# Recurrent attention and a token and channel mixer: padded 512-byte weight pieces, fp32 sums in batch 0, halves read in place, and a stored order table

## The chip, the cores and the metric

The kernel runs on one core of a Trainium2 chip. The metric is the device time of one execution in microseconds (us), from the runs shown below; a trace of one further execution shows what each engine did. The engines are TensorE (PE, with its weight loads as PEld), VectorE (DVE), ScalarE (ACT), GpSimd (POOL) and SyncE (SP), which here only issues transfers (DMAs).

## The reference

There are 4 batches of 768 tokens, with 8 heads of 48 columns, so 384 model columns. Per head a state of 48 by 48 decays by a gate and takes up an outer product at every token:

```python
f = 1.0 / (1.0 + np.exp(-f_logit))
state = f[:, :, t, :, None] * state + np.einsum('bhd,bhe->bhde', k[:, :, t], v[:, :, t])
y[:, :, t] = np.einsum('bhd,bhde->bhe', q[:, :, t], state)
```

The result, heads side by side, is x. It goes through two mixings, first over the tokens and then over the channels:

```python
h = np.maximum(xt @ w_tok1, 0.0) @ w_tok2      # xt: x transposed, hidden 256
u = x + h.transpose(0, 2, 1)
return u + np.maximum(u @ w_ch1, 0.0) @ w_ch2  # hidden 1536
```

All inputs and outputs are fp32.

## The kernel before, in words

**Attention.** Each batch is cut into three chunks of 256 tokens, called b,d (batch, chunk). Two neighbouring tokens lie side by side in one partition (index j in 0, 1), so a chunk fills 128 partitions, and e in 0, 1 names the two halves of 64 partitions. The recurrence is computed in blocks, as masked attention inside a block and a carried state between blocks. For each chunk, with line numbers of the kernel before:

- f is loaded; exp and ln(1 + x) on ACT (L536, L538) give minus the logarithm of the gate. P (L543, DVE) adds the two tokens of a pair into the tile Pf in fp32.
- Pf is split into two bf16 parts: hi, a cast (L545), and lo, the remainder (L547). TensorE forms the running sums of both with a triangular matrix of ones (`cums`, L552: L556 for hi, L557 for lo), and the totals of each half with eight small matmuls (L561, L562). S0 (L566, DVE) takes the second token's value off to get the sums for the first token of each pair.
- G and Gi (L577, L579, ACT) are the exponentials of minus and plus the sums; q and k are multiplied with them ("gating", L607 and L618), transposed on TensorE (L641) or, in batches 2 and 3, by a transposing DMA (L653), and copied out.
- TensorE computes scores (L769, or L725 in batches 2 and 3), DVE multiplies them with a mask (L776, L733), TensorE multiplies with v (L786, L740) and adds the carried state's part (L798, L749). The result is copied to x (L823), and to bf16 for the mixing.

**Mixing.** Token mixing takes two groups of matmuls, tok1 (L839) and tok2 (L855), with the sum u added in place by DVE (L861). u is cast to bf16, transposed on TensorE (L876), and channel mixing follows for two halves of 384 tokens: ch1 (L902) with a relu to the tiles z on ACT or DVE (L909, L911), and ch2 (L927), 12 matmuls into one PSUM bank for each of six tiles of 128 tokens, added to u by DVE (L937). Two stores (L946) put a pair of tiles out, one for each half of the partitions; the last two tiles are stored singly.

**Loads.** SP issues q, k, v and f in one queue, in pieces of 384 bytes (two tokens of one head), into five buffers for each of the four. Behind batch 0's loads stand the token weights in fp32: w1 (L446) in pieces of 2 KB into its own tile w1s, then w2 (L458) in two halves of 3 KB pieces, which borrow one buffer of v and one of k. ACT, POOL and DVE cast them to bf16. The channel weights are loaded, with a cast on the way, in four transfers that POOL issues (L470, L474). The first waits behind a gate (L435) for w2's second half, the third for a load of q of batch 1.

**Order.** Nothing is ordered by hand. Every piece of work is registered with a `Planner`, with its planned time on each engine that may do it, its inputs and outputs, its buffers and a priority. The planner plays the program through: of all work that is ready it takes what can start first by its own clock, and of equal starts the one with the lower priority value (L153). This gives each engine its instruction order, chooses engines and buffers, and is fixed before the kernel runs. The priorities come from due times: 34 us per batch (`due`, `at`, L351 to L373). Where TensorE would idle before 60 us by the plan, filler matmuls on a constant tile (`idle`, L983) are put in; they compute nothing. The PSUM has eight banks; one is kept for fillers until 26 us by the plan (`P.spare`).

Of the kernel before, what the change touches and what calls it, by code (L numbers as in the profile page):

```python
# [12 lines left out]

SEM = 0.06
PE_LAT = 0.10
SW_LEAD, HW_LEAD = 3.9, 3.7


def act_t(n):
    return (0.05 + 0.835e-3 * n, 0.12)  # L20

# [8 lines left out]

def pe_mode(name):

    if name.startswith("sc"):
        return "s"
    if name.startswith("ds"):
        return "d"
    return "v" if name.startswith("av0") else "n"
# [7 lines left out]
class Planner:  # L45


    def __init__(self):
        self.ops, self.by_name = [], {}
        self.pools, self.group_pool, self.group_of = {}, {}, {}  # L50
        self.producers, self.touch = {}, {}
        self.bank_pools, self.banks, self.quota, self.warm = {}, [], None, 0.0
        self.held, self.spare, self.slack, self.patience = [], 0.0, {}, 0.0
# [33 lines left out]
    def run(self):  # L87
# [31 lines left out]
        while ready:  # L119
            best = None  # L120
            cache = {size: self._banks(size) for size in (1, 2)}
            for o in ready:
# [23 lines left out]
                for e, (occ, lat) in o.eng.items():  # L146
# [6 lines left out]
                    key = (round(st + self.patience * max(o.prio, -20.0), 2), o.prio, st + occ)  # L153
# [17 lines left out]
            if o.xfer is not None and e == "POOL":  # L171
# [12 lines left out]
                end = sw + 0.3  # L184
# [50 lines left out]
    def switch(a, b):  # L235
        if a == b:
            return 0.0
        return (0.095 if a == "s" else 0.0) + (0.093 if b != "n" and a != "s" else 0.0)
# [22 lines left out]
def kernel(  # L261
# [23 lines left out]
    XB_FROM = 2  # L285
    DEEP = 2
# [28 lines left out]
    Pf_tiles = [st([128, H, D], FP32, f"Pf{i}") for i in range(2)]  # L315
    P.pool("Pf", Pf_tiles)
    L_tiles = [(st([128, H, 64], BF16, f"Phi{i}"), st([128, H, 64], BF16, f"Plo{i}")) for i in range(2)]
    P.pool("L", L_tiles)
    P.pool("U", [st([128, 2, DM], BF16, f"v_bf{i}") for i in range(3)])
# [8 lines left out]
    idle = st([128, 512], BF16, "idle")  # L328
# [18 lines left out]
    P.patience = 0.0  # L347
    P.spare = 26.0
# [29 lines left out]
    def consts():  # L378
# [4 lines left out]
        for hi, lo in L_tiles:  # L383
            nc.vector.memset(hi[:, :, D:64], 0.0)
            nc.vector.memset(lo[:, :, D:64], 0.0)
        nc.vector.memset(halves, 0.0)
# [6 lines left out]
        nc.vector.tensor_scalar(tri2[0:64, 0:64], tri[0:64, 0:64], -1.0, None, ALU.add)  # L393
        for r in (slice(0, 64), slice(64, 128)):
# [13 lines left out]
    def load(nm, b, d, prio, after=()):  # L408
# [4 lines left out]
             prio, after, xfer=ROW * 128 * H)  # L413

    for b in range(B):
        seq = [(nm, c + 1 if nm == "f" else c) for c in range(-1, NP) for nm in "fqkv"]
        if b == 0:
            seq = [(w[0], int(w[1])) for w in "f0 f1 q0 k0 f2 v0 q1 k1 v1 q2 k2 v2".split()]
# [8 lines left out]
    gates = dict(zip(("wc1a", "wc1b", "wc2a", "wc2b"), ("w2s1", "-", "q1,1", "-")))  # L427
    sw = []

    def sw_dma(nm, outs, fn, n, mb):  # L430
        dep = ["~" + sw[-1]] if sw else []
        at_ = gates.get(nm, "-")
        if at_ != "-":
            P.op(f"gate_{nm}", {"POOL": (0.13, 0.1)}, [at_], [],
                 lambda: nc.gpsimd.tensor_copy(gate_t, P[at_][:, 0, 0, 0:1]), -900 + len(sw), dep)  # L435
            dep = ["~gate_" + nm]
        P.op(nm, {"POOL": (0.7 * n, 0)}, [], outs, fn, -899.5 + len(sw), dep, xfer=mb / 0.31)
        sw.append(nm)
    w1s = st([128, 3, 2, DT], FP32, "w1s")

    def flat(v):
        return P[v].rearrange("p h two d -> p (h two d)")
    tail = f"~ldv0,{NP - 1}"
    for n in range(2):
        P.value(f"w2s{n}", f"w2s{n}", "vk"[n])
    P.op("w1l", {"SP": (0.7, 0)}, [], ["w1s"], lambda: nc.sync.dma_start(  # L446
        out=w1s.rearrange("p g two c -> p g (two c)"),
        in_=moe_w_tok1.rearrange("(g p two) c -> p g (two c)", p=128, two=2)), -400, [tail], xfer=0.786 / 0.35)
    tail = "~w1l"
    for j in range(2):  # L450
        for kk in range(2):
            P.op(f"w1c{j},{kk}", {"POOL": pool_t(768), "ACT": act_t(768)}, ["w1s"], [f"w1{kk}"],
                 lambda e, j=j, kk=kk: cast(
                     e, w_tok1[64 * j:64 * j + 64].rearrange("p (g kk) c -> p kk g c", kk=2)[:, kk],
                     w1s[64 * kk:64 * kk + 64, :, j]), T0 - LEAD - 4 + kk)
    for kt in range(2):
        P.op(f"w2l{kt}", {"SP": (0.7, 0)}, [], [f"w2s{kt}"],
             lambda kt=kt: nc.sync.dma_start(out=flat(f"w2s{kt}"), in_=moe_w_tok2[128 * kt:128 * kt + 128]),  # L458
             -390 + kt, [tail], xfer=0.393 / 0.35)
        tail = f"~w2l{kt}"  # L460
        for th in range(2):
            P.op(f"w2{kt},{th}", {"ACT": act_t(384), "DVE": dve_t(384)}, [f"w2s{kt}"], [f"w2{th}"],
                 lambda e, kt=kt, th=th: cast(
                     e, w_tok2[:, kt, 384 * th:384 * th + 384].rearrange("r (c two p) -> r c two p", two=2, p=64),
                     flat(f"w2s{kt}")[:, 384 * th:384 * th + 384].rearrange(
                         "r (c p two) -> r c two p", p=64, two=2)), T0 - LEAD - 2 + th)
    P.by_name["ldf1,0"].after = (tail,)
    for hf in range(2):
        cols = slice(hf * (DCH // 2), (hf + 1) * (DCH // 2))
        sw_dma("wc1" + "ab"[hf], ["wc1" + "ab"[hf]], lambda cols=cols: nc.gpsimd.dma_start(  # L470
# [550 lines left out]
```

## Time and profile before

The median of 4 runs is 185.09 us (184.31 to 185.58). The profiled execution is one of them.

| | us |
|---|---|
| profiled execution | 185.58 |
| its span, first to last instruction | 183.8 |
| TensorE busy (93%) | 170.8 |
| of it fillers, L983 | 20.7 |
| DVE busy (66%) | 121.5 |
| ACT busy (65%) | 119.7 |
| POOL busy (37%) | 68.0 |

The core moved 31.00 MB at 169 GB/s on average. In the rows shown below, a line such as L902 is a line of the kernel; "out<-in" are tiles with their numbers left out; "issue" is time in which an engine waited for nothing that the profile shows. A share of busy time is an average over stages with different limits, so the stages are read one by one. The chain of waits follows the work that ended last back to the start, in order of time: start, duration, what.

### The profile page before, as it was taken

To read this page: it belongs to the slowest core of one execution; us is meant where nothing else is said; L and a number is where in the kernel's file an instruction comes from. 1 tells how busy PE (TensorE), PEld (TensorE's weight loads), DVE (VectorE), ACT (ScalarE), POOL (GpSimd) and SP (SyncE) were. 2 spreads that over 40 slices of the span, in tenths; PEclk is the share of its full clock that TensorE was granted. 3 is DMA by queue.
4 is the path that set the end of the run, shared out by engine and by line. 5 is a ranking of instruction groups with operands and counts; after the bars stand their busy time and mean duration, and the time that the engine had idled before them with its cause. 6 is when DMAs were issued, how large, how long until landed. Compare 5 with 4: busy or idle time off the path is not lost.

```text
span 183.8 us, 5042 instructions
## 1 busy us (share of the span) xinstructions
PE 170.8 (93%) x2050; PEld 105.9 (58%) x2050; DVE 121.5 (66%) x232; ACT 119.7 (65%) x215; POOL 68.0 (37%) x114
## 2 busy tenths in 40 slices
PE   6899969999999999999989999889999999999990
PEld 2346645575666766565656665356666666566650
DVE  7489865598857688998489996998944266012021
ACT  3879689899766688767777945368337542924800
POOL 3017872375274337385642934437210100000000
PEclk9999997999999999999999999999999999999999
DMA  6999999979993999999999899995352011303033
GB/s 151 261 261 263 294 327 234 209 181 272 209 206 80 278 241 271 205 181 166 207 281 229 176 244 195 198 203 85 44 84 75 0 42 47 86 0 87 4 90 81
DMA packets 69159, 31.00 MB, mean 169 GB/s; under 512 B 63120, under 2 KB 68496, under 8 KB 69136
## 3 DMA queue, kind: packets, MB, share of 16 engines
q1 hardware_dynamic: 66768, 28.32, 72.9%
q0 software_dynamic: 2368, 2.36, 7.7%
q8 instruction: 16, 0.26, 0.6%
q14 instruction: 7, 0.06, 0.1%
HBM read 25.17 MB, written 4.72 MB: 163 GB/s over the span
## 4 chain that ended last, share of the span: by engine, by line
PE 65%; DVE 14%; ACT 7%; SPq 5%; DMA 3%; issue 3%; DVEq 0%; ACTq 0%
PE pp L902 24%; PE pp L927 21%; SPq L412 5%; DVE qkh L618 3%; DMA v_ld<-in_v_dram 3%; DVE xu L861 3%; PE pp L855 2%; PE pp L798 2%; DVE qkh L607 2%; ACT xu L823 2%; PE pp L725 2%; PE pp L839 2%; PE pp L786 2%; PE pp L769 2%; PE pp L641 2%
## 5 line engine op out<-in xcount | busy, mean ns | idle before, releaser
L927 PE MATMUL pp<-w_ch,zT 128*128 128x384 bf16 x288 | 52.2, 326 | 0.0
L902 PE MATMUL pp<-uT,w_ch 128*128 128x384 bf16 x288 | 51.5, 326 | 0.6 <-DVE zT L911 0.4
L909 ACT ACTIVATE zT<-pp 128x384 bf16<-128x384 f32 x72 | 34.9, 491 | 18.1 <-PE pp L902 17.9
L902 PEld LDWEIGHTS <-w_ch 128*128 128x128 bf16 x288 | 26.9, 98 | 17.2 <-issue 1.0
L927 PEld LDWEIGHTS <-zT 128*128 128x128 bf16 x288 | 27.0, 98 | 16.5 <-issue 0.2
L937 DVE TENSOR_TENSOR xu<-xu,pp 128x384 f32<-128x384 f32 x24 | 13.3, 552 | 29.2 <-PE pp L927 29.0
L481 POOL CAST v_bf<-v_ld 64x384 bf16<-64x384 f32 (+1 forms) x28 | 16.2, 579 | 19.4 <-DMA v_ld<-in_v_dram 18.3
L983 PE MATMUL pp<-idle 128*128 128x512 bf16 (+4 forms) x82 | 20.7, 338 | 1.5 <-DVE idle L379 1.5
L776 DVE TENSOR_TENSOR AmT<-pp,msk 128x1024 bf16<-128x1024 f32 x12 | 14.4, 1221 | 3.4 <-PE pp L769 2.1
L911 DVE TENSOR_SCALAR zT<-pp 128x384 bf16<-128x384 f32 x24 | 12.7, 555 | 4.6 <-PE pp L902 3.7
L733 DVE TENSOR_TENSOR AmT<-pp,msk 128x1024 bf16<-128x1024 f32 x12 | 14.1, 1218 | 2.4 <-PE pp L725 2.3
L481 POOL CAST x_bf<-xu 128x768 bf16<-128x768 f32 x10 | 8.5, 852 | 17.7 <-ACT xu L823 17.7
L607 POOL TENSOR_TENSOR qkh<-q_ld,G 128x384 bf16<-128x384 f32 x14 | 13.0, 940 | 2.4 <-ACT glast L574 2.2
L618 DVE TENSOR_TENSOR qkh<-k_ld,pp 64x384 bf16<-64x384 f32 x24 | 13.2, 550 | 0.5
L983 PEld LDWEIGHTS <-idle 128*128 128x128 bf16 x82 | 7.9, 104 | 8.2 <-issue 2.8
L536 ACT ACTIVATE f_ld<-f_ld 128x768 f32<-128x768 f32 x12 | 10.1, 840 | 3.4 <-DMA f_ld<-in_f_logit_dram 3.4
L861 DVE TENSOR_TENSOR xu<-xu,pp 128x384 f32<-128x384 f32 x24 | 11.7, 548 | 0.2 <-PE pp L855 0.2
L548 POOL TENSOR_TENSOR Plo<-Pf,Phi 128x384 bf16<-128x384 f32 x10 | 9.1, 913 | 6.9 <-ACT Phi L479 3.0
L823 ACT COPY xu<-pp 128x768 f32<-128x768 f32 x11 | 8.8, 797 | 4.3 <-PE pp L786 2.3
L577 ACT ACTIVATE G<-pp 128x768 bf16<-128x768 f32 x12 | 9.7, 812 | 2.7 <-DVE pp L566 2.6
L839 PE MATMUL pp<-x_bf,w_tok 128*128 128x384 bf16 x48 | 10.0, 340 | 0.8 <-ACT w_tok L479 0.4
L479 ACT CAST u_bf<-xu 128x768 bf16<-128x768 f32 x8 | 6.5, 831 | 6.3 <-DVE xu L861 6.1
(99 smaller groups left out, 249.1 us busy)
## 6 DMA issues: line engine op xcount, KB each, us to landing
f_ld<-in_f_logit_dram SPq DMA_DIRECT2D x12, 384.0 KB, 5.4
q_ld<-in_q_dram SPq DMA_DIRECT2D x12, 384.0 KB, 6.3
k_ld<-in_k_dram SPq DMA_DIRECT2D x12, 384.0 KB, 6.2
v_ld<-in_v_dram SPq DMA_DIRECT2D x12, 384.0 KB, 6.9
out_dram<-xu SPq DMA_DIRECT2D x22, 192.0 KB, 2.9
w_ch<-in_moe_w_ch_dram POOLq DMA_DIRECT2D x4, 576.0 KB, 9.3
w1s<-in_moe_w_tok_dram SPq DMA_DIRECT2D x1, 768.0 KB, 7.9
v_ld<-in_moe_w_tok_dram SPq DMA_DIRECT2D x1, 384.0 KB, 6.1
```

What stands on the lines that cost most here:

```text
L481: (nc.vector if e == "DVE" else nc.gpsimd).tensor_copy(o, x)
L607: vec(e).tensor_tensor(o, x, g, ALU.mult)
L618: nc.vector.tensor_tensor(o, x, g, ALU.mult)
L733: lambda e=e: nc.vector.tensor_tensor(P[f"Am{e}{i}"], P[f"A{e}{i}"].rearrange("p b (a t) -> p (b a) t", t=128), msk2.rearrange("p j t -> p ...
L776: lambda j=j: nc.vector.tensor_tensor(P[f"Am{j}{i}"], P[f"A{j}{i}"].rearrange("p b (a t) -> p (b a) t", t=128), msk[:, j].rearrange("p j t ...
L839: nc.tensor.matmul(P[f"{g},0"][:, 0:DM], lhsT=w_tok1[:, kt, rt * 128:(rt + 1) * 128], rhs=P[f"xb{b},{kt // 2}"][:, kt % 2], start=(kt == 0 ...
L861: nc.vector.tensor_tensor(x, x, P[f"up{i}"][:, 0:DM], ALU.add)
L902: nc.tensor.matmul(pm, lhsT=w_ch1[:, kt, cc * 128:(cc + 1) * 128], rhs=uT[:, 3 * th:3 * th + 3, kt, :], start=(kt == 0), stop=(kt == 2))
L909: nc.scalar.activation(P[f"z{i}"], P[f"zp{i}"][:, 0:384], AF.Relu)
L927: nc.tensor.matmul(P[f"op{i}"][:, 0:DM], lhsT=P[f"z{b},{th},{cc}"][:, c0:c0 + 128], rhs=w_ch2[:, cc, :], start=(cc == 0), stop=(cc == NCC ...
L937: nc.vector.tensor_tensor(x, x, P[f"op{i}"][:, 0:DM], ALU.add)
L983: nc.tensor.matmul(P.psum_tile[:, bank, 0:n], lhsT=idle[:, 0:128], rhs=idle[:, 0:n], start=True, stop=True)
```

## The change

- **Order.** A table of 967 integers, `RANKS`, replaces the priorities of all registered work, in order of registration. The planner is otherwise the same, with new planned times for several operations (`act_s`, the transposes, the copies of the state, transfers), and keeps a bank for fillers until 30.
- **Token weights.** w1 is loaded by three DMAs, w2 by two, in 512-byte pieces into tiles whose rows are padded from 128 to 132 columns. w2 has its own tile and no longer borrows buffers.
- **Upper halves.** hi is no longer cast: it is the upper 16 bits of Pf, read in place with a step of two bf16 elements. The tiles Phi go, Pf is 64 columns per head.
- **fp32 sums.** In chunks 1 and 2 of batch 0 (`f32p`) the sums are formed by fp32 matmuls from Pf; hi, lo and S0 go there. `minus_ln` starts the first token's sums with minus the second token's value.
- **Tail.** The last tile's ch2 is done in two halves of 192 columns, each with its add. The stores of the last two tiles go out on two queues, SP and ACT.
- **Fillers.** The constant tile is 128 columns; 64 of them are repeated to the filler's width.

Flags that are 0 (`F32`, `WSW`, `COLS`) leave their branches unused. The diff, cut to its core:

```diff
+RANKS = """
+560 561 562 563 564 565 566 567 568 569 570 571 573 574 575 576 577 578 579 580 581 582 583 584 587 588 589 590 591
...
-SW_LEAD, HW_LEAD = 3.9, 3.7
+SW_LEAD, SW_END, HW_LEAD = 2.4, 2.3, 3.7
+def act_s(n):
+    return (0.095 + 0.835e-3 * n, 0.12)
-                    key = (round(st + self.patience * max(o.prio, -20.0), 2), o.prio, st + occ)
+                    key = (int(st * 100.0 + 0.5), o.prio, st + occ)
-                end = sw + 0.3
+                end = sw + SW_END
...
+    HIV = 1
+    F32P = 2
-    Pf_tiles = [st([128, H, D], FP32, f"Pf{i}") for i in range(2)]
+    Pf_tiles = [st([128, H, 64 if HIV else D], FP32, f"Pf{i}") for i in range(2)]
-    idle = st([128, 512], BF16, "idle")
+    idle = st([128, 128], BF16, "idle")
-    P.spare = 26.0
+    P.spare = 30.0
...
+        if F32 or F32P:
+            nc.vector.tensor_copy(tri2f[:, 0], tri2)
+            nc.vector.tensor_copy(halvesf, halves)
+        if F32P:
+            nc.vector.tensor_scalar(tri2f[:, 1], ident, -1.0, None, ALU.mult)
...
-    w1s = st([128, 3, 2, DT], FP32, "w1s")
+        w1s = st([128, 3, 4, 132], FP32, "w1s")
+        def w1_load():
+            for g in range(3):
+                nc.sync.dma_start(out=w1s[:, g, :, 0:128], in_=moe_w_tok1.rearrange(
+                    "(g p two) (ch c) -> g p (two ch) c", p=128, two=2, ch=2)[g])
+        P.op("w1l", {"SP": (1.4, 0)}, [], ["w1s"], w1_load, -400, [tail], xfer=0.786 / 0.33)
...
-             lambda kt=kt: nc.sync.dma_start(out=flat(f"w2s{kt}"), in_=moe_w_tok2[128 * kt:128 * kt + 128]),
+        w2s = st([128, 2, 6, 132], FP32, "w2s")
+                 lambda kt=kt: nc.sync.dma_start(
+                     out=w2s[:, kt, :, 0:128], in_=moe_w_tok2[128 * kt:128 * kt + 128].rearrange("r (c x) -> r c x", x=128)),
...
+        f32p = F32P and b == 0 and d >= F32P - 1
+        def hi_of():
+            if HIV:
+                return P[f"Pf{i}"].bitcast(BF16).rearrange("p h (d two) -> p h d two", two=2)[:, :, :, 1]
+            return P[f"L{i}"][0]
-        P.op(f"hi{i}", {"POOL": pool_t(384), "ACT": act_t(384)}, [f"Pf{i}"], [f"hi{i}"],
+        if not HIV and not f32:
+          P.op(f"hi{i}", {"POOL": pool_t(384), "ACT": act_s(384)}, [f"Pf{i}"], [f"hi{i}"],
...
-            hi, lo = P[f"L{i}"]
+            hi, lo = hi_of(), P[f"L{i}"][1]
+        def minus_ln():
+            nc.tensor.matmul(hd(P[f"S{i}"][:, 0, 0:DM]), lhsT=tri2f[:, 1], rhs=f_()[:, :, 1], start=True, stop=False,
+                             skip_group_check=True)
+
+        def cums32p():
+            x = P[f"Pf{i}"]
+            for a in (1, 0):
+                nc.tensor.matmul(hd(P[f"S{i}"][:, a, 0:DM]), lhsT=tri2f[:, 0], rhs=x[:, :, 0:D], start=(a == 1),
+                                 stop=(a == 0), skip_group_check=True)
+
+        def totals32p():
+            o, x = P[f"S{i}"][:, 1], blk(P[f"Pf{i}"])
+            for hp in range(HP):
+                nc.tensor.matmul(o[:, DM + 2 * hp:DM + 2 * hp + 2], lhsT=x[:, hp], rhs=halvesf, start=False,
+                                 stop=(hp == HP - 1), skip_group_check=True)
+        if f32p:
+            P.op(f"mln{i}", {"PE": (0.65, PE_LAT)}, [f"Ln{i}"], [f"S0{i}"], minus_ln, pg - 3.6)
+            P.op(f"cums{i}", {"PE": (1.3, PE_LAT)}, [f"Pf{i}", f"S0{i}"], [f"S{i}", f"Sa{i}"], cums32p, pg - 3.5)
+            P.op(f"cumt{i}", {"PE": (0.5, PE_LAT)}, [f"Pf{i}", f"Sa{i}"], [f"S1{i}"], totals32p, pg - 3.4)
...
+            if b == B - 1 and tt == NCH - 1:
+                for n in range(2):
+                    c = slice(n * (DM // 2), (n + 1) * (DM // 2))
+                        def ch2(tt=tt, g=g, i=i, th=th, c=c, n=n):
+                            for cc in range(g * 3, g * 3 + 3):
+                                nc.tensor.matmul(P[f"op{i},{n},0"][:, c], lhsT=P[f"z{b},{th},{cc}"][:, c0:c0 + 128],
+                                                 rhs=w_ch2[:, cc, c], start=(cc == 0), stop=(cc == NCC - 1),
+                                                 skip_group_check=True)
+                    def oadd(i=i, s=s, c=c, n=n):
+                        x = P[f"o{i}"][:, s, c]
+                        nc.vector.tensor_tensor(x, x, P[f"op{i},{n},0"][:, c], ALU.add)
...
+                if single:
+                    for j, (q_, e) in enumerate(((nc.sync, "SP"), (nc.scalar, "ACT"))):
+                        P.op(f"out{b},{tts[0]},{j}", {e: (0.6, 0)}, [f"o{b},{tts[0]}"], [],
+                             lambda store=store, j=j, q_=q_: store(js=(j,), eng=q_), due(b, "o", tts[-1]) - 500, xfer=0.45)
...
+    for o, rank in zip(P.ops, RANKS.split()):
+        o.prio = int(rank)
...
-                nc.tensor.matmul(P.psum_tile[:, bank, 0:n], lhsT=idle[:, 0:128], rhs=idle[:, 0:n], start=True,
-                                 stop=True)
+                nc.tensor.matmul(P.psum_tile[:, bank, 0:n].rearrange("p (a c) -> p a c", c=64), lhsT=idle,
+                                 rhs=idle[:, 0:64].unsqueeze(1).broadcast_to((128, n // 64, 64)), start=True, stop=True)
```

## The prediction

> **What bounds the kernel.** I first read the slices of the page, to see where TensorE is short of work.
>
> ```profile
> PE   6899969999999999999989999889999999999990
> ...
> PEclk9999997999999999999999999999999999999999
> DMA  6999999979993999999999899995352011303033
> ```
>
> TensorE looks busy throughout, but the fillers (L983) count as busy. The stages, in the answer by windows, separate them:
>
> ```profile
> 22.10:34.30 12.20, 10.01 (x191) 6.58 (x189) 7.55 (x11) 10.36 (x16) 6.23 (x10) 0.86 1.14 277
> 34.30:41.40 7.10, 6.82 (x78) 4.86 (x77) 5.60 (x12) 7.03 (x13) 4.50 (x6) 1.00 0.88 191
> 41.40:57.70 16.30, 15.88 (x301) 10.35 (x299) 12.87 (x23) 11.94 (x24) 8.17 (x13) 1.00 1.09 212
> 57.70:95.00 37.30, 37.16 (x421) 23.58 (x418) 29.33 (x54) 28.82 (x51) 20.30 (x33) 1.00 1.08 216
> 95.00:125.00 30.00, 27.49 (x357) 17.09 (x356) 27.18 (x47) 18.75 (x36) 14.53 (x25) 1.00 1.07 210
> 125.00:179.20 54.20, 54.19 (x451) 33.10 (x449) 21.53 (x38) 27.52 (x54) 5.52 (x9) 1.00 0.24 51
> ```
>
> The second number is the length, the third TensorE's busy time with its instructions; DVE, ACT and POOL follow after the weight loads, and the clock, DMA share and GB/s end the row. The same stages for the tile idle alone give fillers of 13.69 us before 22.10, then 4.15, 1.21, 1.44, 0.19 and none. So from the first channel matmul (L902, 41.4) to the last (179.2) TensorE has 137.8 us, of which 1.6 us fillers and 0.42 + 0.14 + 2.51 + 0.01 = 3.1 us idle: 133.1 us are work. Before 41.4 it waits for batch 0. The end is therefore "start of the channel stage + 133 + what idles later + tail". The chain of waits shows what sets that start, and the tail:
>
> ```profile
> 24.24 0.30 PE pp L786 x16
> ...
> 26.32 1.02 issue
> ...
> 30.33 0.44 PE pp L786 x16
> 30.77 1.07 PE pp L798 x12
> 31.84 0.32 PE pp L839
> ...
> 32.21 0.48 PE pp L786 x16
> ...
> 41.46 1.06 PE pp L902 x6
> ...
> 56.30 0.62 PE pp L798 x12
> ...
> 173.34 5.86 PE pp L927 x36
> 179.22 0.56 DVE xu L937
> ```
>
> Two accidents stand here: TensorE stopped inside a run of 16 L786 matmuls for 1.02 us with no releaser, and then ran at half clock (the windows of 2 us show 0.85, 0.50, 0.79 from 28 to 34), so that L786 took 0.44 and 0.48 instead of 0.30. Last, the groups that the change removes or replaces:
>
> ```profile
> L607 POOL TENSOR_TENSOR qkh<-k_ld,f_ld 128x384 bf16<-128x384 f32 x2 | 2.0, 994 | 0.0
> L566 DVE TENSOR_TENSOR pp<-pp,f_ld 128x384 f32<-128x384 f32 x12 | 6.7, 562 | 2.4 <-ACT xu L823 1.8 <-PE pp L562 0.4
> L479 ACT CAST Phi<-Pf 128x384 bf16<-128x384 f32 x8 | 4.1, 510 | 3.1 <-DVE Pf L543 2.9
> ```
>
> **What the skill says.** The Trainium skill, DMA: Bandwidth & Descriptors, "Queues, rings and completion order": a DMA engine turns from one queue to another only after a whole packet of several descriptors. The trace fits: instruction fetch has its own queue, the token weights are pieces of 2 and 3 KB, w2's second half lands at 19.66 + 6.6 = 26.26, and the stop lies at 26.32. The trace shows no fetch, so the link is inferred. TensorE: Matmul & The Clock Gate, "What's actually happening": idling halves the clock. The trace agrees in kind (22 to 30 has many gaps, then 0.50). SBUF, "Specifications": full rate needs two hits per 16-byte line; 4-byte steps still give four. No row of before has such a matmul operand.
>
> **The change, part by part.**
>
> *512-byte pieces.* The bytes stay 1.57 MB. Before, the rate rose from 261 GB/s (384-byte pieces) to 396 in 22 to 24 us. I take about 300 for 512 bytes, between those, so 5.2 us instead of some 4.2 us: w2 lands about 1.0 us later (0 to 1.8). Behind it stand the gate of wc1 (27.05), wc1 and batch 1's loads. wc1's two issues at 27.17 and 28.11 land after 7.9 to 10.5 us, by 38.6 at the latest; the delay is hidden as long as channel work starts after some 37 to 39. SP issues three DMAs for w1 instead of one; it was 2.63 us on that one, at a full queue, so I add nothing (0 to 0.5, in front of batch 1's loads, which have slack). Gain: the 1.02 us stop, taken whole (0 to 1.0). w2's own staging also frees one v and one k buffer; the 8.6 us for which SP waited for a buffer of q (POOL L607) is not of these, so I count nothing.
>
> *Upper halves as views.* Twelve casts go: eight of 510 ns on ACT, four of 567 on POOL, 6.3 us. Only the chain to the sums gets shorter, by about 0.55 us per chunk; in the steady stages other TensorE work covers that chain. The price: L556 and L561 read 4-byte steps in the 10 chunks that keep bf16 sums. I take 0; double time would be 0.16 (one 384-column matmul: 5.86/36 us apart) plus at most four 0.05 per chunk, 0.36 x 10 = 3.6 us. A loss only.
>
> *fp32 sums in two chunks of batch 0.* Gone in each: the upper and lower halves (0.51 to 0.75, and 0.56 DVE or 0.91 POOL) and S0 (0.56 DVE). Added on TensorE: three matmuls of 384 and four of 2 columns in fp32. FP8 and Floating Point Precision, "TensorE Precision Notes", has four passes, so an estimate of 4 x 0.163 = 0.65 each, 1.95 us, plus about 0.5, less the 0.53 of bf16: +1.9 us a chunk, 3.8 in all. They fall before about 18 us, where 13.7 us were fillers; with no filler to displace, all 3.8 would count. The chain of chunk 2, Pf to G, was 13.97 to 18.18: POOL 0.75 and 0.91, TensorE 0.7, DVE 0.56. Now it needs about 1.8 us of TensorE. So Gi and the k gating come about 1 us earlier, and with DVE freed the two POOL gatings of 0.99 (21.04 to 22.99) may go to DVE at 0.55. What is late next is v of chunk 2 (cast at 22.10) and the five masks of 1.23. I credit 0.8 (0 to 2).
>
> *Clock.* At full clock the four slow pieces (0.44 + 1.07 + 0.32 + 0.48 = 2.31) are 0.30 + 0.62 + 0.16 + 0.30 = 1.38: 0.93 us. Fewer stops and bank 7 kept for fillers until 30 instead of 26 speak for it; I take 0.7 (0 to 0.9).
>
> *Order table and planner costs.* They move everything and have no row. Bounds for the rest of the program: the 3.1 us idle all gone, or several us more. I take -0.3: 1.78 of the 3.1 lie between 110 and 125, at one join of two batches, where DVE has little room (below).
>
> *Tail.* The last tile is computed in two halves of 192 columns; 24 matmuls at 0.081 are the same 1.95 us (0 to +0.3 if weight loads show). The last add falls from 0.56 to 0.35 (L703's size): -0.2. The two stores, issued on SP until 180.91, go out on SP and ACT at once; Trainium Kernel Development and Optimization, "Key Constraints", says a second issuer saves issue time alone, which is the 0.55 here. ACT's last work ends before 174. Together -0.75 (-0.3 to -0.9).
>
> *Smaller edits.* The narrow filler operand has as many columns to stream. Three added conversions of constants (0.13 each, as L391) hide in the 1.23 us that DVE idles before the first Pf at 6.12; without that cover 0.4.
>
> **Sum.** Start -1.0 - 0.8 - 0.7 = -2.5; later idle -0.3; tail -0.75: -3.55. The profiled execution took 185.58 (span 183.8 and 1.78 around it), so 182.0 for it; it lies 0.49 above the median 185.09, hence 181.5.
>
> **Rivals.**
> - *The loads hold the start (0.20).* DMA is full from 26 to 38 and 44 to 56, wc2's second half lands at about 45.0 + 11.7 = 56.7 and the first L927 is at 57.7. If wc1, wc2 or batch 1 come no earlier, TensorE waits for them and the start's 2.5 shrinks to 0.5: 185.09 - 0.5 - 0.75 = 183.8. Against it: SP stood 8.6 us before 39.52, waiting for a q buffer that earlier gating releases earlier.
> - *It doesn't do what it says (0.08).* The stop just moves, the clock falls again, the tail is eaten by a join: 185.0.
> - *Slower: an uncovered join (0.17).* At the join of batches 2 and 3 a chain mostly on DVE runs from 111.80 (S0) over G, six gatings and six adds to 121.9; from 111.5 to 122 DVE is busy 8.76 of 10.5 us, and TensorE idles only 1.65, because ch2 work (L927) of the batch before and the token matmuls cover the rest. An order that spends this cover early leaves up to 8 us bare. From 4.5 us on (the 3.55, and 0.9 for half a per cent) it decides. At 6 bare: 187.5. For it: the order is fixed from planned times and cannot react. Against: from 57.7 to 95 the same kind of join cost 0.14.
>
> **Chances.** Likeliest 0.55 (181.5, its own range 178.8 to 183.2), loads 0.20, nothing 0.08, join 0.17. Half a per cent, 0.9 us, is about what can be told from no change. Faster: 0.55 and 0.16 of the loads' case, 0.71. Same: 0.04 and 0.08, 0.12. Slower 0.17. The range 178.8 to 186.0 leaves out the bare joins and a start gained by more than 5 us.
>
> **What would show it.** Right: no stop near 26, TensorE's clock at 1.0 throughout, first L902's counterpart at 38 to 39.5, three fp32 matmuls of about 0.65 us apart in chunks 1 and 2, the 384-column strided matmul still 0.16 apart, 3.3 us from last add to the end. Wrong: first channel matmul at 41 or later; strided matmuls at 0.3; idle TensorE above 5 us after the start.

## The result: 184.35 us after 185.09, and the profile after

The changed kernel takes 184.35 us (median; 182.72 to 186.63), the kernel before 185.09. The ratio is 0.9946, with a 95% interval from 0.9929 to 0.9962: 0.74 us were won by the medians where 3.55 were forecast. Ratios, here and below, compare fast executions alone (those within 1.5% of the fastest of the same kernel), so they can differ from the quotient of two medians. The profiled execution took 185.37 us, span 183.6, just 0.2 less than the one before, so the two profiles can be laid side by side: what was won at one place was lost at another. First the slices of the page (tenths of 40 equal parts of the span; PEclk is TensorE's clock):

```profile
PE   7689999989999999959999999989999999999991
...
PEclk9999999999999999996999999999999999999999
DMA  6999999999999899997999799999620000900054
```

The half clock that stood in the seventh slice before is gone. But there is a new gap in TensorE in the 18th slice (from 78 us), and behind it a new drop of the clock. The windows by stage, columns as before (start and end, length, TensorE's busy time with its instructions, weight loads, DVE, ACT, POOL, clock, DMA share, GB/s):

```profile
22.10:34.30 12.20, 12.15 (x222) 7.79 (x214) 9.24 (x14) 10.90 (x18) 6.85 (x11) 1.00 1.04 253
34.30:41.60 7.30, 6.48 (x68) 4.05 (x66) 6.84 (x16) 6.02 (x11) 2.73 (x4) 1.00 1.04 215
41.60:57.00 15.40, 15.40 (x255) 10.26 (x256) 11.34 (x22) 11.98 (x23) 5.88 (x10) 1.00 1.17 229
57.00:95.00 38.00, 35.67 (x444) 22.80 (x443) 27.32 (x47) 26.67 (x48) 16.34 (x28) 0.96 0.93 202
95.00:122.40 27.40, 26.07 (x324) 15.95 (x321) 23.89 (x43) 18.16 (x32) 15.47 (x26) 1.00 1.06 200
122.40:179.50 57.10, 57.01 (x514) 36.14 (x514) 22.43 (x39) 30.79 (x58) 10.18 (x18) 1.00 0.30 70
```

The row from 57 to 95 carries the loss: 2.33 us idle where the same stage had 0.14, and a clock of 0.96, which over 38 us is about 1.5 us. Part of the chain of waits:

```profile
27.55 0.83 POOL w_tok L499
28.44 0.19 POOL gate_t L509
28.63 0.88 POOL w_ch L557
29.51 12.03 DMA w_ch<-in_moe_w_ch_dram
41.59 2.61 PE pp L1043 x15
...
81.87 0.51 POOL v_bf L499
82.42 0.63 PE pp L797 x15
83.05 2.03 PE pp L1043 x6
...
177.48 1.99 PE pp L1071 x24
179.50 0.35 DVE xu L1081
```

L1043 is the first channel matmul's line now (L902 before), and its first group runs from 38.49. There is no stop at 26 any more. The second half of wc1 lands at 41.54, and TensorE waits 0.77 us for it. At 83.05, six L1043 matmuls take 2.03 us, nearly twice their time at full clock (six of 0.163 and a latency of about 0.16): this is the half clock, which the trace has from 82.34 to 85.75. Ahead of it stand the casts of v on POOL, for which TensorE waited 1.14 us before L797, and before these the adds of u on DVE, for which it waited 1.14 as well. Last, the groups that answer to those removed or added:

```profile
L742 POOL TENSOR_TENSOR qkh<-k_ld,f_ld 128x384 bf16<-128x384 f32 x1 | 1.0, 993 | 0.0
L651 PE MATMUL pp<-Pf,tri 128*128 128x384 bf16 x10 | 3.3, 334 | 1.3 <-DVE Pf L632 1.3
L652 PE MATMUL pp<-Plo,tri 128*128 128x384 bf16 x10 | 3.2, 324 | 0.3 <-DVE Plo L643 0.3
L680 PE MATMUL pp<-Pf,tri2f 128*128 128x384 f32 x8 | 3.0, 496 | 0.0
L686 PE MATMUL pp<-halvesf,Pf 128*128 128x2 f32 x16 | 1.9, 241 | 0.0
```

L651 reads the upper halves in steps of 4 bytes and takes 334 ns, L652 the packed lower halves and takes 324. An fp32 matmul appears as two instructions (x8 are four matmuls). The casts to Phi have no row left, and of the two gatings on POOL that the prediction shows as L607 one is left (L742).

From the first channel matmul to the last there are now 141.0 us (38.5 to 179.5) instead of 137.8. Idle time is 0.77 + 2.33 + 1.33 + 0.09 = 4.5 instead of 3.1, the half clock costs 1.5, fillers are about 0.6 us more. These sum to +1.4 + 1.5 + 0.6 = 3.5, against the 3.2 us by which the stretch grew. So the start's 2.9 us are used up, the last matmul ends at 179.5 instead of 179.2, and only the tail, 4.1 us instead of 4.6, remains won.

### The profile page after: what moved, and what is told of

It reads as the page before. It is cut to its first block, busy times and chain, and to the rows that moved or that the text cites. A ratio compares the mean times of both kernels' runs of the same rounds, so it can differ in the third digit from the quotient of the medians.

```text
span 183.6 us, 5051 instructions
## 1 busy us (share of the span) xinstructions
PE 171.4 (93%) x2058; PEld 108.4 (59%) x2058; DVE 118.4 (64%) x226; ACT 118.3 (64%) x209; POOL 64.3 (35%) x114
## 4 chain that ended last, share of the span: by engine, by line
PE 63%; DMA 14%; DVE 10%; POOL 5%; ACT 3%; issue 3%; DVEq 0%; POOLq 0%; ACTq 0%
PE pp L1043 24%; PE pp L1091 20%; DMA w_ch<-in_moe_w_ch_dram 7%; DMA q_ld<-in_q_dram 4%; DVE qkh L753 3%; PE pp L974 2%; PE pp L776 2%; PE pp L996 2%; DMA f_ld<-in_f_logit_dram 2%; DMA out_dram<-xu 2%; POOL w_tok L499 1%; PE pp L904 1%; PE pp L860 1%; POOL v_bf L499 1%; PE pp L1071 1%
## 5 line engine op out<-in xcount | busy, mean ns | idle before, releaser
L1043 PE MATMUL pp<-uT,w_ch 128*128 128x384 bf16 x288 | 52.1, 331 | 0.8 <-DMA w_ch<-in_moe_w_ch_dram 0.8
L1091 PE MATMUL pp<-w_ch,zT 128*128 128x384 bf16 x276 | 51.1, 326 | 0.3 <-DVE xu L1101 0.3
L1050 ACT ACTIVATE zT<-pp 128x384 bf16<-128x384 f32 x79 | 38.5, 492 | 15.3 <-PE pp L1043 14.8
L1043 PEld LDWEIGHTS <-w_ch 128*128 128x128 bf16 x288 | 27.1, 99 | 18.4 <-DMA w_ch<-in_moe_w_ch_dram 0.9
L1091 PEld LDWEIGHTS <-zT 128*128 128x128 bf16 x276 | 25.6, 98 | 15.6 <-issue 0.3
L1154 PE MATMUL pp<-idle 128*128 128x512 bf16 (+5 forms) x70 | 16.8, 323 | 1.1 <-DVE idle L434 1.1
L742 POOL TENSOR_TENSOR qkh<-q_ld,G 128x384 bf16<-128x384 f32 x14 | 13.0, 936 | 6.1 <-ACT G L712 3.4
L643 POOL TENSOR_TENSOR Plo<-Pf 128x384 bf16<-128x384 f32 x9 | 7.4, 826 | 14.3 <-DVE Pf L632 12.9
L499 POOL CAST x_bf<-xu 128x768 bf16<-128x768 f32 x9 | 7.4, 823 | 13.9 <-ACT xu L958 13.6
L497 ACT CAST u_bf<-xu 128x768 bf16<-128x768 f32 x9 | 7.5, 830 | 7.2 <-DVE xu L1002 7.0
L1052 DVE TENSOR_SCALAR zT<-pp 128x384 bf16<-128x384 f32 x17 | 9.1, 556 | 2.2 <-PE pp L1043 1.1
L996 PE MATMUL pp<-h1T,w_tok 128*128 128x384 bf16 x48 | 10.0, 325 | 0.5 <-ACT h1T L979 0.4
L1154 PEld LDWEIGHTS <-idle 128*128 128x128 bf16 x70 | 6.6, 103 | 6.2 <-issue 1.8
```

What stands on the lines that cost most here:

```text
L499: (nc.vector if e == "DVE" else nc.gpsimd).tensor_copy(o, x)
L742: vec(e).tensor_tensor(o, x, g, ALU.mult)
L996: nc.tensor.matmul(pm[:, 0:DM], lhsT=w_tok2[:, kt, tt * 128:(tt + 1) * 128], rhs=P[f"h1{b}"][:, kt, :], start=(kt == 0), stop=(kt == 1))
L1043: nc.tensor.matmul(pm, lhsT=w_ch1[:, kt, cc * 128:(cc + 1) * 128], rhs=uT[:, 3 * th:3 * th + 3, kt, :], start=(kt == 0), stop=(kt == 2))
L1050: nc.scalar.activation(P[f"z{i}"], P[f"zp{i}"][:, 0:384], AF.Relu)
L1091: nc.tensor.matmul(P[f"op{i}"][:, 0:DM], lhsT=P[f"z{b},{th},{cc}"][:, c0:c0 + 128], rhs=w_ch2[:, cc, :], start=(cc == 0), stop=(cc == NCC ...
```

## The experiments

Two accounts stood against each other: that the order laid the join of batches 0 and 1 bare, and the half clock behind it took the gain; or that the loads, with pieces of 512 bytes, gave the start's gain back. All runs compute the whole result; fillers compute nothing. Times are medians, ratios are to executions of the kernel before taken beside each run, with their 95% intervals. The median of these executions lay between 184.67 and 185.08 us, so a difference between two runs of different batches is uncertain by some 0.4 us; where it matters, the difference of the ratios is given too.

**Fillers at the join.**

```diff
+            for _ in range({"uP1,1": 5, "uP1,0": 12, "ds2,1": 18}.get(o.name, 0)):
+                nc.tensor.matmul(P.psum_tile[:, 6, 400:512], lhsT=idle, rhs=idle[:, 0:112], start=True, stop=True,
+                                 skip_group_check=True)
```

> The changed kernel with 35 filler matmuls of 112 columns in unused PSUM columns where TensorE idles between 79 and 82.4 us (5 before the transposes of u pair 1, 12 before those of pair 0, 18 before the state product of chunk 2,1). Theory A (the bare join of batches 0 and 1 gives the start's gain back, in part through the half clock that follows its idling): no window below 0.95 of the clock after 78 us in the profile, and a median some 0.7 us below the changed kernel (about 183.6), since about half of its executions show a lower clock and these are 1.4 us longer. Theory B (the clock falls for another reason, or the dip costs nothing): the same median as the changed kernel, 184.3 to 184.5.

Measured: 183.06 us (182.73 to 183.63), ratio 0.9916 [0.9885, 0.9946]. The windows of the changed kernel, then those of this one:

```profile
78.00:80.00 2.00, 1.65 (x27) 0.92 (x25) 1.96 (x5) 1.68 (x3) 2.00 (x3) 1.00 0.92 124
80.00:82.00 2.00, 0.49 (x6) 0.48 (x7) 1.92 (x5) 1.96 (x5) 1.81 (x5) 1.00 0.94 155
82.00:84.00 2.00, 1.58 (x20) 1.06 (x21) 1.63 (x5) 1.09 (x2) 1.06 (x3) 0.58 0.95 268
84.00:86.00 2.00, 2.00 (x13) 1.30 (x12) 0.42 (x2) 0.98 (x2) 0.69 (x2) 0.56 0.56 132
```

```profile
80.00:82.00 2.00, 1.74 (x41) 1.58 (x39) 1.96 (x6) 1.40 (x4) 1.25 (x3) 1.00 0.91 226
82.00:84.00 2.00, 2.00 (x18) 1.33 (x17) 1.36 (x4) 1.67 (x4) 1.38 (x4) 1.00 0.68 173
84.00:86.00 2.00, 2.00 (x14) 1.17 (x12) 0.34 (x1) 2.00 (x5) 0.00 (x0) 1.00 0.93 198
```

With TensorE kept busy by work that computes nothing, the clock stays at 1.00 and 1.3 us are won by the medians, 0.6 by the ratios. In the changed kernel 2.14 busy us of the 4 from 78 to 82 were followed by 0.58 and 0.56. All six executions with fillers (at most 183.63) are below all of the changed kernel with a lower clock (at least 184.00). That the half clock behind this join costs time is shown, as theory A has it; how much of the gain is clock is taken up with the next run.

**The cover put back.** The same place, with work of the kernel instead of fillers: four groups of ch2 matmuls of batch 0, which the order had spent before 77 us, are moved behind.

```diff
     total = P.run()
+    for n, to in enumerate(("uP1,1", "uP1,1", "uP1,0", "ds2,1")):
+        move((f"ch20,4,{n}",), to)
```

(`move` takes the named pieces of work out of the order and puts them ahead of another.)

> The changed kernel, with the four groups of ch2 matmuls of batch 0's fifth output tile moved in TensorE's order to where the fillers stood: two ahead of the transposition uP1,1, one ahead of uP1,0, one ahead of the state update of chunk 2,1. They are 12 matmuls of 0.163 us, 1.96 us. Theory A (the order left this join no cover; cover lost is idle time gained): TensorE is idle in 57 to 95 us for about 0.5 to 1.0 us instead of 2.33, the clock holds, and the time is 181.9 to 182.6 us, below that of the run with fillers. Theory B (VectorE's and ScalarE's chain of the join sets the pace, TensorE only reaches it earlier): idle stays at 1.8 to 2.4 us, spread before and behind, only the clock's 1.3 to 1.5 us are won in the executions that lost them, and the time is that of the run with fillers, 182.8 to 183.4.

Measured: 182.54 us (182.43 to 182.98), ratio 0.9893 [0.9864, 0.9921], the fastest of all runs. The stage's row:

```profile
57.00:95.00 38.00, 36.06 (x462) 22.97 (x461) 29.20 (x51) 29.03 (x52) 17.48 (x32) 1.00 0.97 212
```

The time is A's, the idle time B's: 1.94 us instead of 2.33, spread over 74 to 82. Most of it ends with ACT (0.88 us for h1T before L996, 0.62 for uT before L797) and with the first add of u on DVE (0.39). From 75.4 to 82 DVE is busy without a gap to speak of (six adds of u of 0.55, four gatings of 0.55, the state's updates), so what is left of the join seems to be set by this chain and not by the cover; that is not shown.

By the medians 1.8 us are won on the changed kernel, by the ratios 1.0. The run with both last stores on SP (below) has the changed kernel's order and, in its trace, a full clock: its last add starts at 177.04, that of this run at 176.73. So 0.3 us are idle time. The clock, which holds in all six executions here (mean clock 0.996 and above), is worth about 0.75: all 42 executions of the changed kernel average 184.25 us, the 20 with a mean clock of 0.995 or more 183.50. What is left of the 1.8 us is not placed; a part of it can be the batch.

**The changed kernel without its table.** The lines that set `o.prio` from `RANKS` are taken out, so that the planner orders by its own priorities.

> The changed kernel without the order table: the priorities from due times, as before, with all the other parts. Theory A (the table spends batch 0's channel work early and leaves the join bare): more of batch 0's second channel matmuls stand after 75 us, TensorE idles under 1 us between 75 and 85, and the time is below the changed kernel, 182.5 to 184. Theory D (the table is what carries the gain): slower than the changed kernel by 1 us or more, 185.5 to 188.

Measured: 185.45 us (185.22 to 186.33), ratio 1.0046 [1.0029, 1.0063]. The rows of the two joins:

```profile
57.00:95.00 38.00, 37.64 (x424) 23.60 (x422) 28.56 (x51) 25.54 (x46) 19.10 (x32) 1.00 1.01 211
95.00:125.00 30.00, 27.43 (x354) 16.72 (x353) 26.69 (x47) 19.67 (x34) 12.43 (x23) 0.94 1.07 206
```

The first channel matmul comes at 38.4 here too: the start's gain is not the table's. 57 to 95 has 0.36 us idle, the join of batches 0 and 1 is covered; 95 to 125 has 2.57, as in the kernel before. So it is the table that moved the bare join from one place to the other, and still it is worth 1.1 us by the medians, 1.9 by the ratios. The time is at the edge of theory D's range. Without the table nothing of the start's gain is left: the last matmul ends at 179.5, and DVE's six adds of u at the join of batches 1 and 2 begin at 118.69 us, where they began at 117.78 in the kernel before.

**Fillers at that other join.** On the kernel without the table.

```diff
+            for _ in range({"av2,2,0": 16, "av2,2,1": 12, "tok22,0": 8, "uP2,0": 8}.get(o.name, 0)):
```

> The changed kernel without its order table, with 44 fillers of 112 columns into unused columns of a bank, which nothing reads, at the join of batches 1 and 2: 16 and 12 ahead of the two output products of chunk 2,2, 8 ahead of the second token matmuls and 8 ahead of the first transposition. Theory A (what a bare join costs beside its idle time is the half clock, wherever the join is): the clock stays full in 110 to 120 us, where the kernel without the table had 0.50 to 0.88 in 112 to 118, and the time falls from 185.45 by 1.0 to 1.8 us to 183.7 to 184.4, faster than before. Theory B (the half clock of that join is not from the idle time): the clock falls there again and the time stays at 185.2 to 185.7.

Measured: 185.43 us (185.21 to 186.73), ratio 1.0038 [1.0017, 1.0059]: nothing. The windows without fillers, then with them:

```profile
112.00:114.00 2.00, 1.42 (x25) 1.04 (x25) 1.57 (x4) 1.20 (x2) 0.55 (x1) 0.88 0.95 130
114.00:116.00 2.00, 2.00 (x8) 0.91 (x6) 1.12 (x3) 1.65 (x4) 1.54 (x3) 0.50 0.82 188
116.00:118.00 2.00, 1.58 (x6) 0.65 (x5) 1.96 (x5) 0.85 (x3) 0.83 (x3) 0.77 1.18 282
```

```profile
112.00:114.00 2.00, 2.00 (x41) 1.59 (x38) 1.58 (x4) 1.11 (x2) 0.40 (x1) 1.00 0.93 129
114.00:116.00 2.00, 1.91 (x12) 0.97 (x10) 1.12 (x3) 1.66 (x4) 1.70 (x3) 1.00 0.85 191
116.00:118.00 2.00, 1.05 (x13) 0.78 (x12) 1.96 (x5) 0.96 (x3) 0.68 (x3) 1.00 1.23 286
```

The clock was kept, as A says, and the time did not follow: both theories miss. TensorE's token matmuls, faster now, only wait longer for DVE, whose six adds of u begin at 118.69 in one and 118.84 in the other. With the fillers TensorE is without work of its own for 1.95 us idle and 2.82 us of fillers in 95 to 125, 4.8 in all, where the kernel before had 2.51 idle: so, as far as these traces tell, this is where the start's gain goes: it waits for DVE.

The executions of the kernel without the table say the same of its half clock: seven with a mean clock of 0.995 or more average 185.40 us, eight at 0.986 or 0.987, of which the profiled one is one, 185.50. (Six at 0.991 take 185.82 to 186.28; none of these has a trace.) So in these two places the half clock was paid for where TensorE's own work came next, behind the join of batches 0 and 1, and was free where DVE's chain set the pace.

**Pieces of 2 and 3 KB in the changed kernel.** w1s and w2s without padding, and whole rows again in the loads of w1 and w2.

> The changed kernel with w1 in pieces of 2 KB and w2 in pieces of 3 KB again, same DMAs and same order. Theory A (large pieces hold up the instruction fetch): TensorE stops again for 0.5 to 1.1 us with no releaser between 25 and 28 us, while w2's second half lands about 1 us earlier than 27.7; first channel matmul no earlier than 38.5; time 0 to 1 us above the changed kernel. Theory C (the pieces only delay the weights): no stop, the gate of wc1 opens up to 1 us earlier, the wait for wc1's second half at 40.8 to 41.6 us goes, time up to 0.8 us below the changed kernel.

Measured: 185.53 us (183.17 to 187.63), ratio 1.0012 [0.9986, 1.0037]. The stop is back, in the chain at the place where it was:

```profile
25.68 0.23 PE pp L904 x5
25.91 0.78 issue
26.68 0.36 PE pp L904 x11
```

The first channel matmul comes at 39.34 instead of 38.49. This is as theory A has it; the time rose by 1.2 us, a little more than A gave.

**The pieces again, on the kernel with the cover.**

> The kernel of the run with the cover moved to the join of batches 0 and 1, with the token weights loaded in rows of 2 and 3 KB again. Theory A (the pieces cure TensorE's stop near 26 us, and this is what they are worth once the join does not hide or add anything): the stop is back, the first channel matmul comes at 39.2 to 39.5 instead of 38.4, and the time rises by 0.7 to 1.1 us to 183.2 to 183.6. Theory B (the later join gives the delay back, since VectorE sets its pace): the first channel matmul is as late, but the last one within 0.3 us of that with pieces, 182.4 to 182.9 us.

Measured: 183.74 us (182.83 to 185.92), ratio 0.9927 [0.9894, 0.9960]. By medians this is 1.2 us slower than with small pieces, as on the changed kernel; by the ratios it is 0.6. The executions divide: nine whose mean clock reads 0.995 or more take 182.83 to 184.23 us, five at 0.991 or less 185.36 to 185.92. The profiled one is of the second kind:

```profile
26.00:28.00 2.00, 1.07 (x21) 0.49 (x24) 0.67 (x1) 1.94 (x5) 1.91 (x3) 0.85 1.20 263
28.00:30.00 2.00, 2.00 (x26) 0.77 (x24) 1.97 (x3) 1.07 (x2) 1.94 (x4) 0.50 1.05 236
30.00:32.00 2.00, 2.00 (x48) 1.58 (x48) 0.73 (x2) 0.18 (x1) 0.09 (x1) 0.79 1.02 205
```

The stop brings the half clock, and the first channel matmul falls to 41.02, 2.5 us later than with small pieces; the last follows by 2.8. Nothing later gives this back, so B is out. The median is just above A's range, which had left the clock out.

**512-byte pieces alone, in the kernel before.** Padded tiles for w1 and w2 as in the change, and its narrow filler tile; order, sums and casts stay, and the plan still sets a buffer of v and one of k aside for w2.

> The kernel before with one part of the change alone: token weights in 512-byte pieces into padded tiles (and the narrow filler tile, to make room), in the order of before. Theory A: the stop of 1.02 us near 26 us is gone and with it the half clock of 28 to 34; w2 lands 0.7 to 1.2 us later; first channel matmul 1 to 2 us before 41.4; time 0.5 to 1.5 us below before. Theory C: the stop stays or the later weights eat it; time within 0.5 us of before or above it.

Measured: 187.97 us (185.56 to 189.82), ratio 1.0130 [1.0068, 1.0192]. TensorE does not stop near 26. But w2 lands at 28.2, wc1 is issued behind it, and a k load of batch 1 is late. In the chain:

```profile
28.19 13.02 DMA k_ld<-in_k_dram
41.33 1.03 DVE qkh L610 x2
```

TensorE's order has the transposes of that k ahead of channel work, and the first channel matmul comes at 43.1. So the pieces alone cost 2.9 us by medians, 2.4 by the ratio, as theory C allows: the stop is gone, but this order stands on loads that now come later.

**wc1 issued earlier.** On the kernel with fillers at the join.

```diff
-("w2s1", "-", "q1,1", "-")
+("w2s0", "-", "q1,1", "-")
+    move(("gate_wc1a", "wc1a"), "w1c1,0")
```

> The kernel of the run with fillers at the join of batches 0 and 1, with one more edit: the gate of wc1's load waits for the first half of w2 instead of the second, and the gate and the issue of wc1's first half stand on POOL ahead of its last cast of w1 rather than behind it. Theory A (POOL's casts hold wc1 back, and TensorE pays for it): the first half of wc1 is issued at about 26.7 us instead of 28.6, its second half lands near 40 instead of 41.5, the wait of 0.77 us at the first channel matmuls goes, the first of them stays at 38.3 to 38.5 and the time falls by 0.5 to 0.8 us against the kernel with the fillers alone, to 182.3 to 182.6 us. Theory B (the DMA engines are full there and the same bytes only share the time otherwise; the last cast of w1, 0.9 us later, holds token mixing instead): the first channel matmul comes 0.3 to 0.9 us later and the time stays at 182.8 to 183.4.

Measured: 182.95 us (182.83 to 183.05), ratio 0.9911 [0.9883, 0.9939], 0.1 below the kernel with fillers, in theory B's range. The first half was issued at 27.5 instead of 28.6, the first channel matmul came at 38.57. There was nothing to win: the kernel with fillers, of the same loads, has no wait for wc1 in its trace either (7.55 of 7.60 us busy in 34 to 41.6), nor have three others with the same start. The 0.77 us belong to the one execution that the page of the changed kernel shows.

**fp32 sums undone, in the kernel with the cover.** The same order; VectorE subtracts again for the low halves and S0, TensorE has the four bf16 sums.

```diff
+            def minus_ln():
+                pass
...
+            def totals32p():
+                nc.vector.tensor_tensor(hd(P[f"S{i}"][:, 0, 0:DM]), hd(P[f"S{i}"][:, 1, 0:DM]), f_()[:, :, 1],
+                                        ALU.subtract)
```

> The kernel of the run with the cover moved to the join of batches 0 and 1, with the fp32 sums of chunks 1 and 2 of batch 0 undone in the same order: VectorE again subtracts for the low halves and for S0 (2 x 0.55 and 2 x 0.57 us more on VectorE), TensorE has the four bf16 sums back (0.53 us a chunk instead of 2.9). Theory A (the prediction's: the sums lie in time that fillers and idle time take anyway, on neither side worth anything): the first channel matmul within 0.3 us of 38.4 and the time within 0.3 us of 182.54. Theory B (VectorE bounds the start, so its 2.2 us of extra work move the first channel matmul): first channel matmul at 38.9 to 40.0, time 183.0 to 184.0. Theory C (the fp32 sums hold TensorE up at the start): first channel matmul 0.4 to 1.0 us earlier and the time 181.5 to 182.2.

Measured: 184.88 us (183.74 to 186.56), ratio 0.9993 [0.9967, 1.0019], 2.3 us slower than with the fp32 sums by the medians and 1.9 by the ratios; the time is above the range of every theory. The first channel matmul comes at 41.02. Then with 14 fillers a chunk in the place of the time that TensorE lost:

```diff
+            def minus_ln():
+                warm(5)
...
+                warm(9)
```

> The kernel of the run without fp32 sums, with 5 fillers of 384 columns where the first fp32 matmul of a chunk stood and 9 behind its bf16 sums (14 x 0.163 = 2.3 us, about what the fp32 sums took more), into the bank that the subtraction for S0 fills afterwards. Theory A (what the fp32 sums give is TensorE's clock: they keep it busy where it otherwise waits, and VectorE's extra work is hidden): the clock is full in 8 to 24 us, where it was 0.50 to 0.85, the first channel matmul comes at 38.4 to 39.0 instead of 41.0, and the time is 182.5 to 183.1. Theory B (what they give is VectorE's 2.2 us): the clock is full, but the first channel matmul comes at 39.5 or later and the time is 183.5 to 184.9.

Measured: 183.95 us (183.30 to 186.54), ratio 0.9965 [0.9942, 0.9987]. Windows of the run without, and of the run with these fillers:

```profile
10.00:12.00 2.00, 1.08 (x8) 0.69 (x8) 1.78 (x4) 1.97 (x6) 0.07 (x1) 0.50 1.28 261
...
20.00:22.00 2.00, 2.00 (x17) 0.83 (x18) 1.36 (x2) 1.50 (x2) 1.86 (x4) 0.50 1.00 263
```

```profile
10.00:12.00 2.00, 1.76 (x15) 0.84 (x13) 1.65 (x4) 1.97 (x6) 0.00 (x0) 1.00 1.29 261
...
20.00:22.00 2.00, 1.88 (x58) 1.15 (x56) 1.49 (x4) 1.34 (x3) 1.92 (x4) 1.00 0.97 281
```

With the fillers the clock is full from 8 to 24 us, and the first channel matmul comes at 39.36, between 41.02 without them and 38.55 with fp32 sums. So the sums do two things: VectorE's shorter chain brings the stage 0.8 us forward (38.55 against 39.36), and their slow matmuls keep the clock up, worth 1.7 us at the start where no filler does it (39.36 against 41.02). In time the two are 1.4 and 0.9 us by the medians, 1.3 and 0.5 by the ratios; it is nearest to theory B, with a part of the gain that A named. The split holds for fillers at these places.

**Both last stores on SP.** First on the changed kernel, then on the one with the cover.

```diff
-                    for j, (q_, e) in enumerate(((nc.sync, "SP"), (nc.scalar, "ACT"))):
+                    for j, (q_, e) in enumerate(((nc.sync, "SP"), (nc.sync, "ACT"))):
```

> The changed kernel with both stores of the last two halves on SP's queue again (the last tile stays split into 192 columns). Theory A (the second queue shortens the tail by about 0.5 us): the last store is issued 0.5 us later, the time from the last matmul to the end of the span is 4.5 to 4.8 us instead of 4.1, and the ratio to the kernel before rises by 0.002 to 0.004. Theory B (the landing takes longer when two queues issue at once, so the issue is won and the landing is lost): the tail is 4.0 to 4.3 us and the time as the changed kernel's, within 0.3 us.

> The kernel of the run with the cover moved to the join of batches 0 and 1, with both last stores on SP's queue. There all executions keep the clock, so the tail can be read from the time. Theory A (the second queue is worth its 0.5 us of issue): 183.0 to 183.2 us, the tail from the last matmul 4.6 us. Theory B (a part of it is lost in landing): 182.7 to 182.9, the tail 4.3 to 4.5. Theory C (all of it is lost): 182.4 to 182.6.

Measured: 184.34 us (183.14 to 185.67), ratio 0.9991 [0.9961, 1.0020], and 183.16 us (182.56 to 183.60), ratio 0.9902 [0.9869, 0.9935]. Rows of the timeline (start, duration), with the cover, then with both stores on SP as well:

```profile
171.96 5.65 SPq L1110 DMA_DIRECT2D out_dram<-xu  x6
...
175.41 2.22 ACTq L1110 DMA_DIRECT2D out_dram<-xu  x2
...
176.73 0.35 DVE L1081 TENSOR_TENSOR xu<-xu,pp 128x192 f32<-128x192 f32 x1 [0.64 <-PE pp L1071]
```

```profile
172.00 6.26 SPq L1110 DMA_DIRECT2D out_dram<-xu  x8
...
176.77 0.35 DVE L1081 TENSOR_TENSOR xu<-xu,pp 128x192 f32<-128x192 f32 x1 [0.64 <-PE pp L1071]
```

Issue ends at 178.26 (172.00 + 6.26) instead of 177.63 (175.41 + 2.22, on ACT), 0.63 later, with a last add 0.04 later; the spans are 181.1 and 180.8. So by these traces the second queue is worth 0.3 us and landing takes the rest, as theory B has it. By the medians it is worth 0.6 on the kernel with the cover, as theory A has it, and nothing on the changed kernel, by the ratios 0.2 and 0.8. The ranges overlap, and how much it is stays open.

## Why the prediction was wrong

Its sum was start -2.5, later idle -0.3, tail -0.75. Step by step:

- **Stop, -1.0: right.** It is gone, and comes back with the large pieces (0.78 us, first channel matmul 0.85 later on the changed kernel). The prediction says that the trace shows no fetch, but it shows some: the page lists a DMA queue q8 of kind instruction with 16 packets, 0.26 MB, one to some 257 of TensorE's matmuls and weight loads. By the traces its second packet starts at 24.90 us in the kernel before, at 24.14 and 24.45 in the two runs that bring the large pieces back, and at 22.36 to 23.76 in ten traces with small ones. (An eleventh, without fp32 sums, has it at 25.60; there TensorE had run at half clock.) In both runs with large pieces in the changed kernel's order TensorE stops behind its 701st matmul or weight load, in the middle of a group of 16. This supports the link with the fetches. It is not shown in full: the packet has landed 0.4 to 0.9 us before the stop begins.
- **Gating of chunk 2, -0.8: right in size.** 38.55 against 39.36, with the clock full in both and both chunks' sums changed. It came with less work on VectorE, as said; one of the two POOL gatings has moved to DVE.
- **Clock, -0.7: right in the profiled execution, wrong as a gain of the median.** The start's clock was full, and the three steps together gave 2.9 us there for 2.5 forecast. But I took the loss of one profiled execution for that of all. Of 42 executions of the kernel before that stand beside the first four runs, 17 have a mean clock of 0.995 or more and take 184.23 us on average; the others take 185.41. And the changed kernel loses as much in about as many, in the traced one elsewhere: 20 of its executions at 0.995 or more average 183.50 us, the 22 below average 184.94. Between executions with a full clock the change is worth 0.7 us, as between the medians. So the clock gave nothing in all.
- **Later idle, -0.3: the step that failed.** In place of a gain of 0.3 the stretch behind the first channel matmul grew by 3.2 us. Idle time after the start rose by 1.4: by 2.2 at the join of batches 0 and 1 and 0.4 at the wait for wc1, less 1.2 at the next join. Behind the first join stood the half clock of 1.5 us in the profiled execution. The rival "uncovered join" has this mechanism, but I placed it at the join at 111 to 122 us (batches 1 and 2 by the tiles' names; the prediction says 2 and 3) on the grounds that 57.7 to 95 had cost 0.14, and priced it by idle time alone. The argument against it was the error: that stretch was covered because the ch2 work of batch 0 reached to 82, and an order of new priorities spends that work earlier (here by 77.1). With the cover back the kernel takes 182.54 us, which is 1.8 of the 2.8 us that were missing by the medians and 1.0 by the ratios. This join still idles 1.94 us; whether that is the rest was not tried.
- **Tail, -0.75: too large.** 4.1 us against 4.6, so -0.5. The last add is 0.35 as said; the store's landing takes back a part of the 0.55 us of issue. The Trainium skill, Trainium Kernel Development and Optimization, "Key Constraints", has a second issuer save the issue time only. The traces show 0.63 us of issue saved, of which 0.3 reach the span; the medians leave the size open.
- **Strided halves, 0: right.** 334 ns against 324, some 0.01 us.
- **fp32 sums, +1.9 us a chunk on TensorE, hidden: right in kind.** Two 384-column matmuls take 1.45 us including a latency of about 0.16, so 0.65 each, as four passes (the Trainium skill, FP8 and Floating Point Precision, "TensorE Precision Notes") make of 0.163. The four totals take 0.79 up to the next matmul, 0.95 with the latency, not 0.5. That these matmuls would also keep the clock up I did not see.
- **Loads.** w2 landed at 27.7, 1.4 us later than 26.26 (1.0 forecast), and the rival of the loads is out for this order: other traces with the same start show no wait for wc1. It is real in the order of the kernel before, where the pieces alone were a loss of 1.3%.

## What to carry to other kernels

A join of two stages that idles little is not safe, it may be covered by work that a new order will spend elsewhere: before trusting it, ask which work covers it and how late that work can go. Price a gap on TensorE with the half clock that may follow, but only where TensorE's own work comes next; at the join here where DVE's chain set the pace, the half clock was free and fillers won nothing. A start that is made shorter can be lost again at the next chain on another engine, as here without the table. And look at the clock of all executions, not of the profiled one, before counting a clock episode as a gain.

## What was not expected of the hardware

The clock falls after scattered gaps, and not every time. The Trainium skill, TensorE: Matmul & The Clock Gate, "What's actually happening", puts it down to an idle window of about 3.4 us that runs freely, not from the kernel's start. The runs agree with the length: the half clock of the kernel before, of the changed kernel and of the kernel without the table lasts 3.41 us in each trace. They agree with the second part: one program has a lower clock in about half of its executions (22 of 42) and is about 1.4 us slower there. On the first part they add that a window of that length need not be empty: in the 3.41 us ahead of the drop TensorE was busy 1.37 us in the changed kernel and 2.06 in the kernel before. Nor is there one busy time that decides: with the cover and large pieces the clock fell after 2.29 busy us of 3.41 (24.00 to 27.41), while the run of the changed order with both stores on SP kept a full clock though TensorE was busy for only 1.87 of the 4 us from 78 to 82. With the cover the clock held in all six executions, with 2.80 of 4 at the leanest place (74 to 78), as far as the mean clock tells. An fp32 weight load takes 192 ns instead of 97.
